# Pooled attention and a two-layer network on one core: one level of Strassen's scheme in the first product

## The chip, the core and the metric

The kernel runs on one core of one Trainium2 chip. Metric: device microseconds of one execution. The kernel before takes 949.67 us, the median of three runs (948.38 to 950.49). Engines are named as in the profile: PE multiplies matrices, PEld is its loading of the stationary operand, DVE, ACT and POOL work on vectors, SP issues the transfers.

## The reference, cut to what matters

Eight batches of eight heads, 576 positions, 64 features a head; keys and values are averaged over groups of 8 positions. The attention's output is a matrix x of 4608 tokens by 512, and goes through a network of width 2048:

```python
h = x @ w_in                                   # 4608x512 times 512x2048: "the first product"
sp = np.maximum(h, 0.0) + np.log1p(np.exp(-np.abs(h)))
g = h * erf(sp)
return (g @ w_out).astype(np.float32)          # 4608x2048 times 2048x512: "the second product"
```

The kernel computes both products with split operands: a float32 matrix is cut into a high part (rounded to the type `fp32r`) and a low part (the rest), and three products of parts are added up: high by high, high by low, low by high.

## The kernel before, in words

Tokens are cut into nine chunks of 512 (`TC`), the width of 2048 into sixteen pieces of 128 (`ft`). Each weight comes as 64-bit floats (`wi`, `wo`), one piece of 128x512 in one transfer of 512 KB. `load_weights` turns it into a high and a low part: two ACT or POOL steps (lines 340, 345, 347), two DVE steps (349, 351), a rounding copy (302 on ACT or 303 on POOL) and a subtraction on POOL (356). All 32 converted pieces stay in on-chip memory for the rest of the run.

`job` does the attention for a block of up to 256 tokens, tile by tile of up to 128 tokens: scores (PE, line 431), maximum and subtraction (DVE 436, 452), exponential (ACT 456), sum (DVE 458), normalization (DVE or POOL 472: both of its operands are in on-chip memory), transposes (PE 479, 484), and the values' products (PE 510, 511), whose results are split into `xh` and `xl` (516, 518).

`pair` handles two steps, each a chunk and one `ft`. The first product has 12 matrix instructions of 512 columns (line 535: four blocks of the 512 features, three products of parts each). Its result is copied out of the bank (540 on DVE or 541 on ACT), goes through softplus and erf (553, 560, each after a load of an ACT table), is multiplied (563) and split again into `gh` and `gl` (565 on ACT; 568 on DVE or POOL). The second product has 12 matrix instructions as well (line 582); `gh` and `gl` are the stationary operand there, and it adds up over the sixteen `ft` in four banks. So first and second products take turns, 12 by 12, and a chunk has 192 of each. `store` writes a finished chunk through two buffers `f` (594, 595, 596).

The order of all this is laid down before the kernel runs. `Program.order` plans with a cost in ns for each operation, a priority and a limited number of buffers, and places each operation where it can start first; the engines then run their instructions in that order, and wait for each other by semaphores. While PE has nothing to do in the first 57 us of the plan, it inserts idle matrix instructions ("fillers", line 622). Up to `FILL` they stand where the plan has a gap.

Of the kernel before, what the change touches and what calls it, by code (L numbers as in the profile page):

```python
# [39 lines left out]
SHIFT = 4  # L40
B1 = 2
# [5 lines left out]
W_IN, W_OUT, L_DUE = -1.0, -2.0, 2.0  # L47
G2 = 5.0
ON_DVE = 2
CAP_H, CAP_O, CAP_ATT, CAP_CV = 2, 4, 4, 2  # L50
ON_ACT = (0,)
SLACK, BIAS = 30, 2000
# [3 lines left out]
SWITCH = 1300  # L56
C_ID = 0
# [37 lines left out]
class Buf:  # L95


    def __init__(self, pool, shape, dtype, tag, limits):
        self.args = (pool, shape, dtype, tag)
        self.limits = limits  # L100
        self.left = 0
        self.state = {}
        self.held = False
        self._ap = None

    @property
    def ap(self):
        if self._ap is None:
            pool, shape, dtype, tag = self.args
            self._ap = (pool() if callable(pool) else pool).tile(shape, dtype, tag=tag, name=tag)  # L110
        return self._ap


class Op:
    def __init__(self, eng, cost, prio, fn):
        self.eng, self.cost, self.prio, self.fn = eng, cost, prio, fn
        self.bufs, self.next, self.wait, self.ready = [], [], 0, 0.0
        self.set = None


class Program:
# [9 lines left out]
    SAME = {"PE": 0, "ACT": 130, "DVE": 130, "POOL": 105, "SP": 0}  # L131

    def __init__(self, capacity, window):
        self.ops, self.capacity, self.window, self.filler = [], capacity, window, None

    def op(self, eng, cost, prio, fn, reads=(), writes=(), hold=(), alt=None, funcs=None):
# [3 lines left out]
        o.set = funcs  # L140
# [23 lines left out]
        for d, flow in deps.items():  # L164
            d.next.append((o, flow))
            o.wait += 1
        self.ops.append(o)
        return o

    def order(self):  # L170
        free = {e: 0.0 for e in self.DELAY}
        free["SP"] = 2150.0
        slots = {t: [0.0] * n for t, n in self.capacity.items()}
# [6 lines left out]
        progress, out, loaded = 0.0, [], "sigmoid"  # L180
        spare = heapq.heappop(slots["banks"]) if self.filler else None
        for _ in self.ops:
            best = None
            for e, ops in avail.items():
                pick, ready = None, []
                for o in ops:
# [4 lines left out]
                    start += switch  # L191
                    need = {}
# [5 lines left out]
                    for t, k in need.items():  # L198
# [3 lines left out]
                        start = max(start, heapq.nsmallest(k, slots[t])[-1] + (DGE if e == "SP" else 0))  # L202
                    if ok and e != o.eng:
                        ok = start + o.choice[e][0] <= max(o.ready, free[o.eng]) + o.cost + BIAS
                    if ok:
                        ready.append((start, o.key, o, start - switch * (1 - TURN) + SLACK * o.prio))
# [4 lines left out]
            if best is None:  # L211
                raise RuntimeError("no operation can go on")
# [5 lines left out]
            if spare is not None and o.eng == "PE":  # L218
                if start > FILL:
                    heapq.heappush(slots["banks"], start)  # L220
# [5 lines left out]
            if o.eng == "PE":  # L226
                progress = max(progress, o.prio)
            for b in o.bufs:
                if not b.held:
                    b.held = True  # L230
                    for t in b.limits:
                        heapq.heappop(slots[t])
                b.left -= 1
                b.end = max(getattr(b, "end", 0.0), end)
                if not b.left:
                    for t in b.limits:
                        heapq.heappush(slots[t], b.end + 150)
# [10 lines left out]
            out.append(o)  # L248
        self.length = max(free.values())
# [11 lines left out]
def moe_attention(ctx: ExitStack, tc: tile.TileContext, cst, qa, kl, vl, wi, wo, out):  # L261
# [3 lines left out]
    if wide:  # L265
# [5 lines left out]
    sizes = {"xh": 2, "xl": 2, "raw": 2, "q": 2, "et": 1, "etb": 1,  # L271
             "s": 2, "m": 2, "z": 2, "bb": 1, "ks": 1, "vs": 1, "hs": 3, "y": 1, "f": 2, "gh": 3, "gl": 3}
    pools = {t: pool(t, n) for t, n in sizes.items()}
    banks = pool("banks", 8, space=PSUM)
    sizes.update({"banks": 8, "h": CAP_H, "o": CAP_O, "att": CAP_ATT, "cv": CAP_CV})
# [3 lines left out]
    def buf(tag, shape, dtype=F32):  # L279
        return Buf(pools[tag], [P] + shape, dtype, tag, [tag])  # L280

    def bank(kind):
        return Buf(banks, [P, 512], F32, "banks", ["banks", kind])

# [7 lines left out]
    def gps(n):  # L292
        return 2.5 * n + 110

    def both(pool_too, cost, pool_cost, prio, fn, *access):

        op("DVE", cost, prio, lambda: fn(nc.vector), *access,
           alt=("POOL", pool_cost, lambda: fn(nc.gpsimd)) if pool_too else None)

    def copy(pool_too, n, prio, dst, src, *access, scale=1.0):  # L300

        op("ACT", act(n), prio, lambda: nc.scalar.activation(dst(), src(), AF.Copy, scale=scale), *access,
           alt=("POOL", 0.833 * n + 161, lambda: nc.gpsimd.tensor_scalar(
               out=dst(), in0=src(), scalar1=scale, scalar2=0.0, op0=ALU.mult, op1=ALU.add)) if pool_too else None)

# [9 lines left out]

    weights = pool("weights", 1)
    sizes.update({f"{n}{ft}": 1 for n in ("wi", "wo") for ft in range(NJ)})
    pieces = lambda n: [Buf(weights, [P, 2, 512], F32R, f"{n}{ft}", [f"{n}{ft}"]) for ft in range(NJ)]
    w_in, w_out = pieces("wi"), pieces("wo")
# [5 lines left out]
    def f32(ap):  # L325
        return ap.bitcast(F32)

    def load_weights(src, w, due):

        n = 512  # L330
        f, raw = buf("f", [n]), Buf(weights, [P, n, 2], U32, w.args[3], w.limits)
        words = lambda i: raw.ap[:, :, i]
        wh, wl = (lambda: w.ap[:, 0]), (lambda: w.ap[:, 1])
        if wide:


            op("SP", 1900, due - 6, lambda: nc.sync.dma_start(raw.ap.rearrange("p f w -> p (f w)"), src), [], [raw])
# [4 lines left out]

            low = buf("hs", [n], U32)
# [9 lines left out]
        else:  # L353
            op("SP", 950, due - 6, lambda: nc.sync.dma_start(f.ap, src), [], [f])
        copy(True, n, due - 2.5, wh, lambda: f.ap, [f], [(w, 0)])
# [307 lines left out]
```

## Time and profile before

| | |
|---|---|
| median of the runs shown | 949.67 us |
| profiled execution, own time | 950.75 us |
| its span | 949.0 us |
| PE busy | 928.5 us, 98% |
| ACT busy | 632.7 us, 67% |
| DVE busy | 445.9 us, 47% |
| POOL busy | 282.9 us, 30% |
| moved by the transfers | 58.55 MB |

The span is from the first to the last instruction; 1.75 us of the execution lie around it. A matrix instruction is pipelined: the next one starts before the last has ended, so what a matrix instruction costs is read from the distance between starts, not from its own duration. Idle time of an engine that nobody waits for costs nothing.

### The profile page before, as it was taken

The numbers are of one execution on the slowest core, as the hardware profiler recorded it, in microseconds if no ns is written. First come the engines' busy times: TensorE is split into PE (matmuls) and PEld (weight loads), VectorE is DVE, ScalarE is ACT, GpSimd is POOL, SyncE is SP. The second block draws the span as 40 slices with busy tenths as digits, with TensorE's granted clock in tenths as the row PEclk, the third lists the DMA queues.
The fourth block names the chain that finished last, engine by engine and source line by source line (L and its number), as shares of the span: only waits on it lengthen the run. The fifth ranks groups of instructions, "written<-read, shape, count | busy, mean of one in ns | idle before, by whom it ended". The sixth has DMA issues, their size and how long they took to land.

```text
span 949.0 us, 12377 instructions
## 1 busy us (share of the span) xinstructions
PE 928.5 (98%) x4485; PEld 767.2 (81%) x4485; DVE 445.9 (47%) x873; ACT 632.7 (67%) x1028; POOL 282.9 (30%) x400
## 2 busy tenths in 40 slices
PE   8999989999999999999999999999999999999997
PEld 6787767888888888888888888888888888888886
DVE  6987775543454444443455444434444443323331
ACT  5888775866675666766666667766666666666653
POOL 2689874241045301451132502242111010101000
PEclk9999999999999999999999999999999999999999
DMA  7892212310032100310021101120100010001001
GB/s 263 292 403 104 80 45 62 94 35 12 12 100 71 31 12 23 117 50 12 6 95 56 46 12 56 61 67 17 51 23 12 12 45 1 1 1 45 1 1 45
DMA packets 30349, 58.55 MB, mean 62 GB/s; under 512 B 7120, under 2 KB 7248, under 8 KB 30288
## 3 DMA queue, kind: packets, MB, share of 16 engines
q1 hardware_dynamic: 30288, 57.75, 18.5%
q8 instruction: 36, 0.59, 0.3%
q14 instruction: 25, 0.20, 0.1%
HBM read 48.30 MB, written 9.44 MB: 61 GB/s over the span
## 4 chain that ended last, share of the span: by engine, by line
PE 86%; DVE 1%; ACT 1%; DMA 0%; issue 0%; POOL 0%; ACTq 0%
PE banks L582 39%; PE banks L535 38%; PE banks L431 3%; PE banks L510 3%; PE banks L479 1%; PE banks L511 1%; DVE s L472 0%; PE banks L484 0%; DMA out<-f 0%; ACT hs L345 0%; ACT L553 0%; DVE m L436 0%; DVE s L452 0%; ACT y L553 0%; ACT banks L340 0%
## 5 line engine op out<-in xcount | busy, mean ns | idle before, releaser
L535 PE MATMUL banks<-xh,wi 128*128 128x512 f32 x1152 | 382.3, 393 | 1.4 <-DVE y L563 1.3
L582 PE MATMUL banks<-wo,gh 128*128 128x512 f32 x1152 | 362.0, 395 | 0.0
L535 PEld LDWEIGHTS banks<-xh,wi 128*128 128x128 f32 x1152 | 217.8, 189 | 48.8 <-DVE y L563 2.8
L582 PEld LDWEIGHTS banks<-wo,gh 128*128 128x128 f32 x1152 | 210.5, 188 | 42.4 <-issue 1.2
L535 PE MATMUL banks<-xl,wi 128*128 128x512 f32 x576 | 225.4, 391 | 0.0
L582 PE MATMUL banks<-wo,gl 128*128 128x512 f32 x576 | 224.9, 390 | 0.0
L541 ACT COPY hs<-banks 128x512 f32<-128x512 f32 x89 | 52.2, 586 | 202.1 <-PE banks L535 200.7
L568 DVE TENSOR_TENSOR gl<-hs,gh 128x512 fp32r<-128x512 f32 x78 | 55.3, 711 | 175.7 <-ACT gh L565 173.3
L582 PEld LDWEIGHTS banks<-wo,gl 128*128 128x128 f32 x576 | 108.1, 188 | 23.5
L535 PEld LDWEIGHTS banks<-xl,wi 128*128 128x128 f32 x576 | 108.9, 189 | 22.5
L568 POOL TENSOR_TENSOR gl<-hs,gh 128x512 fp32r<-128x512 f32 x50 | 64.6, 1292 | 184.6 <-ACT gh L565 174.4
L563 DVE TENSOR_TENSOR hs<-y,hs 128x512 f32<-128x512 f32 x128 | 87.7, 727 | 42.4 <-ACT y L560 42.2
L565 ACT CAST gh<-hs 128x512 fp32r<-128x512 f32 x128 | 78.6, 614 | 37.2 <-PE banks L582 32.7
L436 DVE TENSOR_REDUCE m<-banks 128x4 f32<-128x288 f32 (+1 forms) x80 | 36.2, 455 | 128.3 <-PE banks L431 127.2
L553 ACT ACT_TABLE_LOAD x72 | 92.4, 1283 | 1.8 <-PE banks L535 0.6
L560 ACT ACT_TABLE_LOAD x70 | 89.8, 1283 | 1.2
L494 POOL TENSOR_SCALAR etb<-etb 32x256 fp32r<-32x256 f32 (+1 forms) x40 | 22.4, 561 | 199.2 <-ACT etb L489 116.0
L560 ACT ACTIVATE y<-y 128x1024 f32<-128x1024 f32 (+1 forms) x73 | 76.5, 1049 | 0.8
L553 ACT ACTIVATE y<-hs 128x512 f32<-128x512 f32 x128 | 73.9, 625 | 0.7
L468 POOL TENSOR_TENSOR bb<-s,z 128x64 f32<-128x64 f32 (+1 forms) x40 | 12.2, 306 | 157.2 <-DVE z L462 149.3
L540 DVE COPY hs<-banks 128x512 f32<-128x512 f32 x39 | 27.0, 692 | 65.7 <-PE banks L535 65.7
L381 POOL TENSOR_TENSOR raw<-raw 128x256 f32<-128x256 f32 (+1 forms) x60 | 47.2, 790 | 25.0 <-DMA raw<-vl 13.3
(76 smaller groups left out, 935.5 us busy)
## 6 DMA issues: line engine op xcount, KB each, us to landing
raw<-vl SPq DMA_DIRECT2D x42, 256.0 KB, 2.8
out<-f SPq DMA_DIRECT2D x36, 256.0 KB, 2.0
raw<-kl SPq DMA_DIRECT2D x30, 288.0 KB, 3.1
wi<-wi SPq DMA_DIRECT2D x16, 512.0 KB, 8.1
wo<-wo SPq DMA_DIRECT2D x16, 512.0 KB, 9.4
q<-qa SPq DMA_DIRECT2D x28, 256.0 KB, 2.7
hs<-qa SPq DMA_DIRECT2D x4, 256.0 KB, 5.1
q<-qa SPq DMA_DIRECT2D x8, 128.0 KB, 2.5
```

What stands on the lines that cost most here:

```text
L381: op("POOL", gps(4 * size), prio, lambda: nc.gpsimd.tensor_add(t.ap[:, 0:4], t.ap[:, 0:4], t.ap[:, 4:8]), [t], [t])
L431: nc.tensor.matmul(o, raw.ap[:, p, :T], kbd[:, p], start=(pp == 0), stop=True, skip_group_check=True)
L436: op("DVE", dve(4 * SP), r + 0.4, lambda pv=pv, gs=gs: nc.vector.tensor_reduce(m.ap[:T, gs], pv(), AX.X, ALU.max), [ps], [(m, g)])
L510: nc.tensor.matmul(o, va[:, p], et.ap[:, p, :n], start=True, stop=False, skip_group_check=True)
L535: nc.tensor.matmul(ph.ap, w_in[ft].ap[:, w, P * p:P * p + P], x.ap[:, p, :], start=(p == 0 and q == 0), stop=(p == NP - 1 and q == 2))
L541: [ph], [hs[u]], alt=("ACT", act(TC, True), lambda u=u, ph=ph: nc.scalar.copy(hs[u].ap, ph.ap)))
L553: nc.scalar.activation(y.ap[:, half(k)], hh[k].ap, AF.Softplus)
L560: op("ACT", act(w), n + 1.9, lambda sl=sl: nc.scalar.activation(y.ap[:, sl], y.ap[:, sl], AF.Erf), own, own, funcs="sigmoid")
L563: op("DVE", dve(TC), n + 1.9, lambda k=k: nc.vector.tensor_mul(g(k), y.ap[:, half(k)], hh[k].ap), [(y, k), hh[k]], [gs[k]])
L565: op("ACT", act(TC), n + 2.0, lambda k=k: nc.scalar.copy(gh[k].ap, g(k)), [gs[k]], [gh[k]])
L568: e.tensor_sub(gl[k].ap, g(k), f32(gh[k].ap))
L582: nc.tensor.matmul(o[t].ap, g.ap[:, gs], w_out[ft].ap[:, w], start=(ft == 0 and q == 0), stop=(ft == NJ - 1 and q == 2))
```

## The change

Chunk 0 is computed as before, but with all sixteen `ft` of the first product ahead of the second product. The other eight chunks go in four pairs. Let A11, A12 be the two halves (256 features each) of the weights of piece i, and A21, A22 those of piece i+8; B11, B21 the two halves of the features of the pair's first chunk, B12, B22 those of its second. One level of Strassen's scheme in Winograd's form computes the four blocks of the result with seven products of half the depth where eight would be needed (`quad`, eight for each pair of chunks). Each of the seven is 6 matrix instructions of 512 columns: 42 for a quad, where the kernel before has 48.

- The sums of weights (S1 to S4, `sums`) and of features (T1 to T4, `sides`) are formed in float32 and then split into high and low parts. The attention's result is therefore kept in float32 (`xr`), and split later, in `limbs`.
- Five additions for each quad put the products together, all on DVE (`add`, line 733), with one operand in a bank; the first block of the four is read out of its bank directly by softplus.
- Softplus and erf take four blocks at once, so that the ACT tables change half as often.
- The second product is a phase of its own, after the eight quads of a pair, and transposed: the weights are the stationary operand and the tokens the moving one. It has 12 matrix instructions for each `ft` and chunk, as before. The result is written transposed, and the host turns it round.
- Weights no longer stay on the chip. Once converted, the parts are written to main memory (`raw_hbm`, `in_hbm`, `sum_hbm`, `out_hbm`), and every use loads them anew in pieces of 256 KB, high and low parts (`piece`, 14 places): seven for a quad, and two for each step of the second product.
- Buffers: 87 places of 2 KB a partition for all kinds of tile, instead of a pool for each.
- The planner now also counts POOL and those DVE operations marked `port` as one resource that only one of them can use at a time.

```diff
+NQ = NJ // 2
+FIRST, LONG, SHORT, PERIOD = 17.5, 14.0, 20.5, 34.5
+CAPS = {"g": 32, "x": 28, "xr": 11, "w": 14, "ws": 8, "w0": 36, "gl": 8, "t": 6, "f": 3, "q": 2, "q0": 4, "f0": 14, "v": 3, "vm": 1, "low": 2, "sw": 8,
+        "h": 6, "o": 4, "att": 4, "cv": 2, "dl": 3}
...
+                    if e == "POOL" or (e == "DVE" and o.port):
+                        start = max(start, port)
...
+    def halves(src, hi, lo, prio, reads, hikey, lokey, n=512, turn=None):
+
+        copy(True, n, prio, hi, src, reads, [hikey], [lokey[0] if isinstance(lokey, tuple) else lokey], turn=turn)
+        both(True, dve(n), gps(n), prio + 0.1, lambda e: e.tensor_sub(lo(), src(), f32(hi())),
+             reads + [hikey], [lokey])
...
+    def load_in(ft, due):
+
+        f, hi, lo = convert(wi[ft], due)
+        op("SP", 720, due + STORE, lambda: nc.sync.dma_start(raw_hbm[ft], f.ap), [f], [RAW[ft]])
+        a = slice(0, 2) if ft < NQ else slice(1, 2)
+        for l, w in enumerate((hi, lo)):
+            op("SP", 720 if ft < NQ else 360, due + STORE + 1, lambda l=l, w=w: nc.sync.dma_start(
+                f32(in_hbm[ft][:, a, l]), f32(w.ap).rearrange("p (a f) -> p a f", a=2)[:, a]), [w], [(IN[ft], l)])
...
+    def piece(src, kept, due, shape=(2, 256)):
+
+        w = place("w", F32R, shape)
+        op("SP", 720, due - 2, lambda: nc.sync.dma_start(f32(w.ap), f32(src())), [kept], [w], turn="w")
+        return w
...
+    def sides(s, due):
...
+                less(b[k], a[k], t1, q, sl, u)
+                less(b[2 + k], b[k], t3, q + 0.1, sl, u)
+                less(b[2 + k], t1, t2, q + 0.2, sl, u)
+                limbs("T2", k, t2, q + 0.3, sl, u)
+                limbs("T3", k, t3, q + 0.4, sl, u)
+                limbs("T1", k, t1, q + 0.5, sl, u)
+                less(a[2 + k], t2, t4, q + 0.6, sl, u)
+                limbs("T4", k, t4, q + 0.7, sl, u)
+                limbs("B22", k, b[2 + k], q + 0.8, sl, u)
...
-            def gemm1(ph=ph, ft=ft, xh=xh, xl=xl):
-                for p in range(NP):
-                    for q, (w, x) in enumerate(((0, xh), (0, xl), (1, xh))):
-                        nc.tensor.matmul(ph.ap, w_in[ft].ap[:, w, P * p:P * p + P], x.ap[:, p, :],
-                                         start=(p == 0 and q == 0), stop=(p == NP - 1 and q == 2))
...
+        p1, v, u = place("t"), place("t"), place("t")
...
+        product(A, a11, "B11", False, False)
+        out_of_bank(512, due + 0.3, lambda: p1.ap, lambda: A.ap, [A], [p1])
+        product(Bk, s2, "T2", False, True)
+        add(v, p1, Bk, due + 0.6)
+        product(C, s3, "T3", False, False)
+        add(u, v, C, due + 0.8)
+        product(Dk, s1, "T1", False, False)
+        add(g[1, 1], u, Dk, due + 1.0)
+        product(C, a22, "T4", True, True)
+        add(g[1, 0], v, C, due + 1.6)
+        product(A, a12, "B21", True, True)
+        product(Dk, s4, "B22", True, True)
+        add(g[0, 1], v, Dk, due + 1.8)
...
+    def second(ck, k, due, weights):
...
+            def gemm(j0=j0, o=po[ck]):
+                for j in (j0, j0 + 1):
+                    sl = slice(P * j, P * j + P)
+                    three(o[j].ap, (wh.ap[:, sl], wl.ap[:, sl]), (gh.ap, gl.ap), k == 0, k == NJ - 1)
```

**Three places in the order.** The first is PE in chunk 0. Before, PE has done the first product of two pieces of `wi` (`wi_545` is the second), and then the values' products of a block take turns with 53 fillers (one LDWEIGHTS and one MATMUL each) until the third piece comes:

```order
L535 MATMUL banks<-xh,wi_545 128x512
L510 MATMUL banks<-et,va 128x64
L511 MATMUL banks<-etb,vb 64x64
L510 MATMUL banks<-et,va 128x64
L511 MATMUL banks<-etb,vb 64x64
L622 LDWEIGHTS cst
L622 MATMUL banks<-cst 128x256
```

Now, from the first piece (high part `w_506`, low part `w_529`) to the second and third, there are no fillers in between:

```order
L664 MATMUL h<-x,w_506 128x512 x2
L664 MATMUL h<-x,w_529 128x512
L664 MATMUL h<-x,w_519 128x512 x2
L664 MATMUL h<-x,w_557 128x512
...
L664 MATMUL h<-x,w_613 128x512 x2
L664 MATMUL h<-x,w_627 128x512
```

What moved: 53 fillers that stood after PE's first matrix instruction of the first product are gone, and the conversion of `wo` has moved behind that of `wi`.

The second place is DVE at the start of the first pair, between its first product (which needs only B11) and its second (which needs T2, the end of the chain through `xr`). Line 638 forms the T's, line 349 the low parts (`x` of features, `ws` of weight sums), line 576 belongs to the last tile of attention, 430 and 431 to the sums of weights, 733 is the first addition of a quad:

```order
L576 TENSOR_TENSOR etb<-att,etb 32x128 x2
L431 TENSOR_TENSOR sw<-sw 128x256
L430 TENSOR_TENSOR sw<-sw 128x256
L638 TENSOR_TENSOR xr<-xr 128x128 x2
L638 TENSOR_TENSOR xr<-xr 128x384 x2
L638 TENSOR_TENSOR xr<-xr 128x128 x2
L638 TENSOR_TENSOR xr<-xr 128x384
L349 TENSOR_TENSOR x<-xr,x 128x384 x3
L638 TENSOR_TENSOR xr<-xr 128x128 x2
L638 TENSOR_TENSOR xr<-xr 128x384
L349 TENSOR_TENSOR x<-xr,x 128x128 x2
```

Nothing of this stands in the order before; there, DVE only splits the attention's result (line 518, one instruction for each values' product). What moved: the T's and their low parts now stand between the last tile of attention and PE's next product.

The third place is SP. Before, from chunk 2 on, it issues nothing but the attention's inputs and the outputs:

```order
L420 DMA q<-qa 128x512 x4
L596 DMA out<-f 128x512 x4
L375 DMA raw<-kl 128x576 x4
L420 DMA q<-qa 128x512
L375 DMA raw<-vl 128x512 x6
```

Now, in the first product of the second pair, the weights of each quad (`wi` the plain parts, `ws` the sums), and then those of the second product with the attention's inputs between them:

```order
L444 DMA w<-wi_84 128x512
L444 DMA w<-wi_92 128x512
L444 DMA w<-ws_140 128x512
L505 DMA q<-qa 128x512
L444 DMA w<-wo_141 128x512 x2
L460 DMA raw<-kl 128x576
L444 DMA w<-wo_149 128x512 x2
```

What moved: the whole program issues 765 transfers with 206.6 MB instead of 189 with 57.7 MB, all in SP's one queue.

More of the change, by code (lines that the diff above doesn't have):

```diff
@@ L56 @@
 SWITCH = 1300
+PLACES = 87
 C_ID = 0
@@ L166, in op @@
             o.wait += 1
+        if turn is not None:
+            if turn in self.turns:
+                self.turns[turn].follow.append(o)
+                o.wait += 1
+            self.turns[turn] = o
         self.ops.append(o)
@@ L179, in order @@
                     avail[e].append(o)
-        progress, out, loaded = 0.0, [], "sigmoid"
-        spare = heapq.heappop(slots["banks"]) if self.filler else None
+        todo = [(o.prio, i, o) for i, o in enumerate(self.ops) if o.eng == "PE"]
+        heapq.heapify(todo)
+        progress, out, loaded = todo[0][0], [], "sigmoid"
+        spare = None
+        if self.filler:
+            spare = heapq.heappop(slots["bank"])
+            self.idle.place = spare[1]
         for _ in self.ops:
@@ L225, in order @@
             end = free[o.eng] = start + o.cost
-            if o.eng == "PE":
-                progress = max(progress, o.prio)
+            if e == "POOL" or (e == "DVE" and o.port):
+                port = end
+            o.done = True
+            while todo and todo[0][2].done:
+                heapq.heappop(todo)
+            progress = todo[0][0] if todo else progress
             for b in o.bufs:
@@ L236, in order @@
                     for t in b.limits:
-                        heapq.heappush(slots[t], b.end + 150)
+                        heapq.heappush(slots[t], (b.end + 150, b.places[t]))
+            for d in o.follow:
+                d.wait -= 1
+                if not d.wait:
+                    for a in d.choice:
+                        avail[a].append(d)
             for d, flow in o.next:
@@ L388, in job @@
             for p in range(NP):
-                load_pool(kl[b, p], ks, p, SP, base + KEYS + KEYS_R * p, "s" if first and p > 1 else "raw")
+                load_pool(kl[b, p], ks, p, SP, base + KEYS + KEYS_R * p, "raw")
             for r0, c0 in ((64, 0), (0, SP)):
@@ L501, in job @@
             at += T
-        xh, xl = xtile(ck)
         xs = slice(off, off + n)
+        plain = ck == 0
+        if ck not in xt:
+            if plain:
+                xt[ck] = [(place("x", F32R), place("x", F32R)) for _ in range(NP)]
+            else:
+                xt[ck] = [place("xr") for _ in range(NP)]
         for p in range(NP):
@@ new lines, in three, with activation, softplus @@
+    def three(o, w, x, first, last):
+        (wh, wl), (xh, xl) = w, x
+        for q, (u, v) in enumerate(((wh, xh), (wh, xl), (wl, xh))):
+            nc.tensor.matmul(o, u, v, start=first and q == 0, stop=last and q == 2, skip_group_check=True)
+    def activation(hs, prio):
+        ys = [buf("d", [2, 512]) for _ in range(2)]
+        y = lambda k: ys[k // 2].ap[:, k % 2]
+        own = [(ys[k // 2], k % 2) for k in range(4)]
+        def softplus():
+            for k, (h, _) in enumerate(hs):
+                nc.scalar.activation(y(k), h.ap, AF.Softplus)
+        op("ACT", 4 * act(512), prio, softplus, [h for h, _ in hs], own, funcs="softplus")
+        for k in range(2):
+            op("ACT", act(1024), prio + 0.2, lambda k=k: nc.scalar.activation(ys[k].ap, ys[k].ap, AF.Erf),
+               own[2 * k:2 * k + 2], own[2 * k:2 * k + 2], funcs="sigmoid")
+        for k, (h, g) in enumerate(hs):
+            if g is h:
+                both(True, dve(512), gps(512), prio + 0.3, lambda e, k=k, h=h: e.tensor_mul(
+                    h.ap, y(k), h.ap), [own[k], h], [h])
+            else:
+                op("DVE", dve(512), prio + 0.3, lambda k=k, h=h, g=g: nc.vector.tensor_mul(
+                    g.ap, y(k), h.ap), [own[k], h], [g])
@@ L592, in store @@
-    def store(ck, t, o, prio):
-        ot, r0 = buf("f", [DM]), TC * ck + P * t
-        op("ACT", act(512, True), prio, lambda: nc.scalar.copy(ot.ap, o.ap), [o], [ot],
-           alt=("DVE", dve(512), lambda: nc.vector.tensor_copy(ot.ap, o.ap)))
-        op("SP", 800, prio, lambda: nc.sync.dma_start(out[r0:r0 + P, :], ot.ap), [ot], [])
-    steps = [(ck, ft) for ck in range(NC) for ft in range(NJ)]
-    loads = sorted([(ft + W_IN, wi[ft], w_in[ft]) for ft in range(NJ)]
-                     + [(ft + G2 + W_OUT, wo[ft], w_out[ft]) for ft in range(NJ)], key=lambda w: w[0])
@@ L603, in moe_attention @@
+    gs, po = {}, {}
+    order = [i + NQ * m for i in range(NQ) for m in range(2)]
+    start = lambda s: FIRST + PERIOD * (s - 1)
+    jobs = {}
     for ck, b, tiles, off, fresh in blocks():
```

350 lines of the change are left out of this document (217 added, 133 removed).

## The prediction

> **What bounds the kernel now.** I read the page's first two parts, then a table of stretches with the busy time of each engine, then the chain of waits at the end, which gives the price of a matrix instruction.
>
> ```profile
> PE 928.5 (98%) x4485; PEld 767.2 (81%) x4485; DVE 445.9 (47%) x873; ACT 632.7 (67%) x1028; POOL 282.9 (30%) x400
> ...
> 200.00:400.00 200.00, 200.00 (x956) 165.91 (x955) 87.45 (x178) 133.13 (x210) 54.53 (x80) 1.00 0.14 42
> 250.00:930.00 680.00, 680.00 (x3204) 564.11 (x3203) 282.62 (x556) 444.85 (x674) 146.47 (x216) 1.00 0.11 36
> ...
> 928.70 13.61 PE banks L582 x60
> ```
>
> The columns of a stretch are PE, PEld, DVE, ACT and POOL busy, the granted clock, the share of the transfer engines and GB/s. From 250 to 930 us PE is never idle, at full clock, and no other engine is busy for more than 65%. So there the time is PE's work and nothing else. In the last chain 60 matrix instructions take 13.61 us: **226.8 ns each**. The first product, the second product and the attention's scores in the same stretch:
>
> ```profile
> 39.39:150.00 110.61, 49.14 (x191) 37.30 (x192) 0.97 0.47 167
> 250.00:930.00 680.00, 323.64 (x1343) 251.21 (x1341) 1.00 0.11 36
> ...
> 39.39:150.00 110.61, 35.71 (x144) 26.54 (x144) 0.97 0.47 167
> 250.00:930.00 680.00, 337.29 (x1339) 247.04 (x1340) 1.00 0.11 36
> ...
> 39.39:150.00 110.61, 7.97 (x48) 6.37 (x48) 0.97 0.47 167
> 250.00:930.00 680.00, 29.53 (x200) 26.11 (x200) 1.00 0.11 36
> ```
>
> The 2682 instructions of both products take 608.3 of the 680 us. The other 71.7 us are attention, 25 tiles by their 200 score instructions: **2.87 us a tile**.
>
> The first 150 us are different. PE's first product starts at 39.39 us. Until 150.0 it does 336 instructions (76.2 us) and 6 tiles (17.2 us) in 110.6 us, so **17.2 us are lost** there. The rows below show where.
>
> ```profile
> 50.24 3.67 PE L622 MATMUL banks<-cst 128*128 128x256 bf16 x32
> ...
> 60.90:150.00 89.10, 79.98 (x354) 63.67 (x354) 64.50 (x113) 70.22 (x106) 71.00 (x90) 0.96 0.35 118
> ...
> 120.33 1.31 POOL L356 TENSOR_TENSOR wo<-f,wo 128x512 fp32r<-128x512 f32 x1
> 120.42 0.69 DVE L351 SCALAR_TENSOR_TENSOR f<-wo,banks 128x512 uint32<-128x512 uint32 x1 [0.48 <-POOL wi L356]
> 122.44 1.27 POOL L356 TENSOR_TENSOR wo<-f,wo 128x512 fp32r<-128x512 f32 x1
> 122.52 4.42 DVE L472 TENSOR_TENSOR s<-s,z 64x576 f32<-64x576 f32 x1
> 124.64 1.27 POOL L356 TENSOR_TENSOR wo<-f,wo 128x512 fp32r<-128x512 f32 x1
> 125.87 0.45 POOL L383 TENSOR_TENSOR raw<-raw 128x128 f32<-128x128 f32 x1
> 128.18 0.43 PE L479 MATMUL banks<-cst,s 64*128 64x64 f32 x4 [3.01 <-DVE s L452]
> 129.41 0.63 PE L535 MATMUL banks<-xl,wi 128*128 128x512 f32 x1
> 129.84 1.05 PE L535 MATMUL banks<-xh,wi 128*128 128x512 f32 x2
> L472 DVE TENSOR_TENSOR s<-s,z x34: 741/759/4423, 55.7 to 804.1; 128x576 f32<-128x576 f32 x27, 64x576 f32<-64x576 f32 x7
> ```
>
> PE idles in fillers before the third weight, since conversion isn't ready. Later POOL is the busiest engine (71.0 of 89.1 us) and DVE gets stuck behind it: line 472, with both operands on chip, takes 759 ns in the median and 4.42 us while POOL has no gap, whereas line 351, with one operand in a bank, takes its 0.69 us beside a running POOL instruction. PE then stands for 3.01 us, and its next instructions start 0.43 us apart (129.41 to 129.84) for 3.4 us: a stall of that length costs about 1.7 us more.
>
> **The change, term by term.** The sum is made on the span, 949.0 us; the profiled execution's own time is 1.75 us more, the median shown 0.67 us more, and I use the median.
>
> *Removed.* The order has 1344 instructions in the pairs' first products instead of 1536, 192 in chunk 0 and 1728 in the second product as before. PE has 192 fewer by 226.8 ns: **-43.5 us**. The transposed product has operands of the same size, so the same price. No row of before has steady products beside transfers at a high rate (36 GB/s from 250 to 930); that arriving weights slow PE's step is possible, and I charge nothing for it.
>
> *End.* Now two buffers `f` hold the last stores up:
>
> ```profile
> 943.27 0.39 PE L582 MATMUL banks<-wo,gl 128*128 128x512 f32 x1
> 944.39 0.59 ACT L594 COPY f<-banks 128x512 f32<-128x512 f32 x1 [2.15 <-DMA out<-f]
> 945.31 0.59 ACT L594 COPY f<-banks 128x512 f32<-128x512 f32 x1 [0.33 <-DMA out<-f]
> ```
>
> The last copy ends at 945.90. With a third buffer and one copy each on ACT and DVE it ends some 0.9 us after PE's 943.66: **-1.3 us**.
>
> *Start and first pair.* Ahead of the first product the order has the same work on DVE, ACT and SP, so I leave 39.39 us as it is. Then four sections, priced by these rows (mean ns of one behind the busy time):
>
> ```profile
> L568 DVE TENSOR_TENSOR gl<-hs,gh 128x512 fp32r<-128x512 f32 x78 | 55.3, 711 | 175.7 <-ACT gh L565 173.3
> L568 POOL TENSOR_TENSOR gl<-hs,gh 128x512 fp32r<-128x512 f32 x50 | 64.6, 1292 | 184.6 <-ACT gh L565 174.4
> L303 POOL TENSOR_SCALAR wi<-f 128x512 fp32r<-128x512 f32 x13 | 8.5, 655 | 1.3 <-DVE f L351 1.0
> L381 POOL TENSOR_TENSOR raw<-raw 128x256 f32<-128x256 f32 (+1 forms) x60 | 47.2, 790 | 25.0 <-DMA raw<-vl 13.3
> L518 DVE TENSOR_TENSOR xl<-banks,xh 128x256 fp32r<-128x256 f32 (+3 forms) x96 | 32.6, 351 | 14.7 <-ACT xh L516 13.6
> ...
> 5.00:10.00 5.00, 4.73 (x37) 3.70 (x34) 2.59 (x4) 0.86 (x2) 0.00 (x0) 1.00 1.03 353
> ```
>
> 1. Instructions 1 to 48 (10.9 us of PE): only `wi` is converted, the fillers are gone. Between 10.9 and 13; I take 12, since DVE has 11.8 us of work here.
> 2. 49 to 384, the rest of chunk 0: PE has 76.2 us and 8 tiles, 99.2 us. POOL has 32 subtractions at 1.29 (41.3), 22 rounding or byte steps at 0.66 (14.4) and 32.9 us of pooling and small steps: 88.6. DVE's operations with both operands on chip add 18.4 (11 of 512 columns, 4 normalizations, 5 of 384, the rest small). If these exclude POOL as at 122.52, that is 107.0 us in a row. Before, from 60.9 to 150, the same two kinds filled some 80 of 89.1 us, 90%; at 90% this section takes 119. Bounds 99 and 119; I take 113, for the planner now keeps the two apart, yet ACT (90.8) and DVE (92.1) are nearly as full.
> 3. The first 48 of pair 1: PE has 10.9 and 1.9 us. Its second product waits for T2. DVE, whose queue holds the T's, low parts and weight sums, has 18 low parts of 128 or 384 columns (7.0), 9 of weight sums (3.4), 13 T's (4.9), 5 additions (3.5), 7 sums (2.7) and 0.9 besides: 22.4 us, and POOL little. Bounds 13 and 24; 22.5, since PE waits for that very queue.
> 4. The next 96: PE 21.8 us. The queue has 10.0 MB, stores of weights included; at the 353 GB/s of the saturated row it needs 28.3. Bounds 21.8 and 29; 25, as nobody waits for most of the stores.
>
> Lost in the four: 1.1 + 13.8 + 9.7 + 3.2 = 27.8 us, against 17.2 before: **+10.6 us**.
>
> A rule of the Trainium skill bears on section 2, the page "SBUF — State Buffer", section "Who interferes with whom": a DVE instruction with two SBUF inputs and a GpSimd instruction that reads SBUF exclude each other for their whole length, others do not. The trace agrees (4.42 us at line 472, 0.69 at line 351). By the rule section 2 can't be shorter than 107.0; without it 99.2 would do and the forecast be 14 us lower.
>
> *The quads.* Each has five additions with a bank as operand, and the fifth product writes into the bank that the second addition must have read. From the third product's last start that addition ends 0.39 + 0.04 + 0.69 us later, by these rows:
>
> ```profile
> 922.87 0.39 PE L535 MATMUL banks<-xh,wi 128*128 128x512 f32 x1
> 923.30 0.69 DVE L540 COPY hs<-banks 128x512 f32<-128x512 f32 x1 [1.15 <-PE banks L535]
> ```
>
> The fourth product covers 0.23 + 1.36 us. That leaves some 0.4, unless an unrelated DVE instruction of 0.7 us is ahead. Bounds 0 and 0.7 us a quad; with 0.1, 32 quads give **+3.2 us**. In a pair's first product (76.2 us) ACT has 7.5 us a quad of 9.5, so the activation stays hidden, with half the table loads; its cover is the next quad.
>
> *Streaming.* A pair issues 41.2 MB, 117 us at 353 GB/s, of 189 us of PE (720 x 0.2268 + 9 tiles). Fourteen places hold 19 us of work ahead; a transfer lands in 2 to 10 us here:
>
> ```profile
> raw<-vl SPq DMA_DIRECT2D x42, 256.0 KB, 2.8
> wo<-wo SPq DMA_DIRECT2D x16, 512.0 KB, 9.4
> ```
>
> Nothing is charged. Stores and inputs of attention are queued behind the pieces, and they wait in turn; the same 19 us cover that.
>
> Sum: 949.67 - 43.5 - 1.3 + 10.6 + 3.2 = 918.7, so **919 us**. Its own range, 909 to 930, comes from 103 to 119 in section 2 and 0 to 0.25 us a quad.
>
> **Rivals.**
>
> *The start costs no more than before.* Section 2 at its 107 and 3 at 22 us, with nothing lost in 1, 4 and the quads: lost 7.8 + 9.2 = 17, as before: 949.67 - 44.8 = 905 us. For it: the planner's new exclusion. Against it: no section before ran at full use of its busiest engine.
>
> *The start eats most of it.* 13, 119, 24 and 29: lost 2.1 + 19.8 + 11.2 + 7.2 = 40.3, and 0.35 us a quad, 11.2: 949.67 - 44.8 + 23.1 + 11.2 = 939 us. For it: POOL, DVE, ACT, PE and the queue are all within 15% of one another in section 2, and each stall over 3 us halves the clock.
>
> *Streaming binds, slower than before.* One queue in order, 206.6 MB instead of 57.7, stores mixed in. PE waits once the queue yields under 41.2 MB / 189 us = 218 GB/s, and all is lost under 208 (9 us more a pair, in 3.5 pairs). At half the row of 353, 234 us a pair: 919 + 3.5 x 45 = about 1077. Against it: 353 in the row at 5 us, with lines of 2 KB; for it only that no row before holds a mix of reads and writes at such a rate.
>
> That PE's instructions don't get fewer is excluded by the order.
>
> **How the numbers follow.** Forecast 0.50, costless start 0.21, costly start 0.21, streaming 0.06, and 0.02 for a result between 940 and 950 by several of these. Range 904 to 940: it takes in both starts and leaves out the streaming. Measurements of this kernel tell 0.2% (2 us) from no change. Faster 0.92, same 0.02, slower 0.06.
>
> **What would show it.** PE 3264 instructions of 512 columns at 227 ns; PE busy throughout a later pair, and a pair's period near 189 us; DVE in a row of instructions with PE idle for about 10 us at the start of pair 1; POOL and DVE nearly full in chunk 0. I am wrong if PE waits for `w` pieces in pairs 2 to 4, if each quad has a gap over 0.3 us, or if the first product starts much later than 39 us.

## The result, and the profile after

The changed kernel takes **914.78 us** in the median of four runs (912.97 to 915.98), the kernel before 949.56; the ratio is 0.9633, with a 95% interval of 0.9612 to 0.9653. The forecast was 919, its range 904 to 940. The profiled execution took 915.39 us, with a span of 913.6. Of all executions in this document one was far slower, one of the six of experiment 7 (1269.57 us, at a mean granted clock of 0.653 where the others have 0.99); the ratios leave it out, and without it that median is 909.0 instead of 909.1 us.

The first part of the page, then the product instructions in the stretches of the prediction's sections (from the first to the 49th, 385th, 433rd, 529th and the last one; the columns are PE, PEld, clock, share of the transfer engines, GB/s), and the end of the chain:

```profile
PE 890.5 (97%) x4250; PEld 729.2 (80%) x4250; DVE 554.6 (61%) x1036; ACT 507.4 (56%) x898; POOL 415.1 (45%) x538
```

```profile
40.06:51.05 10.99, 10.99 (x49) 9.10 (x50) 1.00 0.48 167
51.05:158.95 107.90, 84.79 (x337) 62.20 (x336) 0.98 0.89 303
158.95:186.05 27.10, 16.50 (x48) 11.76 (x49) 0.75 1.00 352
186.05:208.10 22.05, 22.05 (x98) 18.02 (x96) 1.00 0.95 353
208.10:909.39 701.29, 650.42 (x2737) 506.36 (x2735) 1.00 0.60 205
```

```profile
744.37 77.37 PE h L664 x336
821.73 88.07 PE o L664 x384
```

Three things are to be seen. The start (the first four rows) takes 168.0 us, of which 27.1 belong to the first 48 instructions of pair 1. From 208 us on PE never stands still: the eight quads of the last pair are one row of 336 instructions without a gap. And that row gives 230.3 ns for an instruction, the second product 229.3, where the row that gave the price had 226.8. Streamed weights land in a median of 5.3 us, and PE has no wait for them among its waits:

```profile
w<-wo SPq DMA_DIRECT2D x256, 256.0 KB, 5.3
w<-wi SPq DMA_DIRECT2D x96, 256.0 KB, 5.2
w<-ws SPq DMA_DIRECT2D x96, 256.0 KB, 5.3
```

At the start of pair 1 PE and DVE stand as follows (timeline, the start and the time of a row, in brackets the idle time ahead and what ended it):

```profile
166.53 0.79 PE L664 MATMUL h<-x,ws 128*128 128x512 f32 x1 [2.14 <-ACT x L337]
169.13 1.65 PE L664 MATMUL h<-x,ws 128*128 128x512 f32 x3 [1.81 <-DVE x L349]
171.37 5.36 PE L664 MATMUL h<-x,ws 128*128 128x512 f32 x14 [0.59 <-DVE x L349]
178.89 4.55 PE L664 MATMUL h<-x,w 128*128 128x512 f32 x12 [2.17 <-issue]
```

```profile
164.31 2.29 DVE L638 TENSOR_TENSOR xr<-xr 128x128 f32<-128x128 f32 x7
166.52 1.48 DVE L349 TENSOR_TENSOR x<-xr,x 128x384 fp32r<-128x384 f32 x3
...
171.03 2.54 DVE L349 TENSOR_TENSOR x<-xr,x 128x128 fp32r<-128x128 f32 x5
...
175.72 1.42 DVE L349 TENSOR_TENSOR ws<-sw,ws 128x256 fp32r<-128x256 f32 x4
...
178.11 0.68 DVE L733 TENSOR_TENSOR t<-t,h 128x512 f32<-128x512 f32 x1
```

DVE goes from T's to low parts to weight sums to the quad's first additions, PE waits for this row four times (the first time by way of ACT, which rounds the T's), and the clock is at half for half of the section (mean 0.75). The last of the four waits, ahead of the fifth product, ends 0.10 us after the second addition (178.11 + 0.68 us). That addition must have read the bank into which the fifth product writes, and it stands in DVE's row behind the weight sums. The profile names no releaser for it ("issue").

### The profile page after: what moved, and what is told of

It reads as the page before. It is cut to its first block, busy times and chain, and to the rows that moved or that the text cites. A ratio compares the mean times of both kernels' runs of the same rounds, so it can differ in the third digit from the quotient of the medians.

```text
span 913.6 us, 13356 instructions
## 1 busy us (share of the span) xinstructions
PE 890.5 (97%) x4250; PEld 729.2 (80%) x4250; DVE 554.6 (61%) x1036; ACT 507.4 (56%) x898; POOL 415.1 (45%) x538
## 4 chain that ended last, share of the span: by engine, by line
PE 88%; DVE 4%; POOL 4%; issue 2%; DMA 1%; ACT 1%; SPq 0%; POOLq 0%; DVEq 0%; ACTq 0%
PE o L664 42%; PE h L664 35%; PE att L516 4%; PE att L599 3%; PE h L816 2%; PE att L564 2%; POOL w L349 1%; PE att L600 1%; DMA v<-vl 1%; POOL low L390 1%; DVE f L394 1%; DVE x L349 0%; DMA wi<-w 0%; PE att L569 0%; DVE xr L638 0%
## 5 line engine op out<-in xcount | busy, mean ns | idle before, releaser
L664 PE MATMUL o<-gl,w 128*128 128x512 f32 x1728 | 425.3, 396 | 0.0
L664 PEld LDWEIGHTS o<-gl,w 128*128 128x128 f32 x1728 | 315.7, 188 | 67.6 <-issue 1.0
L664 PE MATMUL h<-x,w 128*128 128x512 f32 x1344 | 315.8, 395 | 5.2 <-DVE g L685 3.0
L664 PEld LDWEIGHTS h<-x,w 128*128 128x128 f32 x1344 | 254.0, 189 | 62.3 <-DVE g L685 3.4
L682 POOL TENSOR_TENSOR g<-d,g 128x512 f32<-128x512 f32 x54 | 69.6, 1306 | 192.5 <-ACT d L678 192.5
L733 DVE TENSOR_TENSOR g<-t,h 128x512 f32<-128x512 f32 x96 | 65.9, 686 | 61.0 <-PE h L664 59.4
L349 POOL TENSOR_TENSOR gl<-g,gl 128x512 fp32r<-128x512 f32 x62 | 87.4, 1410 | 33.0 <-ACT gl L337 31.6
L337 ACT ACTIVATE gl<-g 128x512 fp32r<-128x512 f32 x119 | 70.8, 623 | 19.8 <-DVE g L685 17.3
L733 DVE TENSOR_TENSOR t<-t,h 128x512 f32<-128x512 f32 x64 | 43.9, 687 | 56.3 <-PE h L664 50.4
L678 ACT ACTIVATE d<-d 128x1024 f32<-128x1024 f32 x72 | 72.5, 1053 | 0.4
L349 DVE TENSOR_TENSOR gl<-g,gl 128x512 fp32r<-128x512 f32 x82 | 57.3, 721 | 13.9 <-ACT gl L337 9.9
L343 ACT COPY f<-o 128x512 f32<-128x512 f32 x21 | 12.2, 587 | 84.9 <-PE o L664 84.7
```

The costliest lines, as they stand in the source:

```text
L343: op("ACT", act(n, True), prio, lambda: nc.scalar.copy(dst(), src()), *access, alt=("DVE", dve(n), lambda: nc.vector.tensor_copy(dst(), sr ...
L349: both(True, dve(n), gps(n), prio + 0.1, lambda e: e.tensor_sub(lo(), src(), f32(hi())), reads + [hikey], [lokey])
L664: nc.tensor.matmul(o, u, v, start=first and q == 0, stop=last and q == 2, skip_group_check=True)
L678: op("ACT", act(1024), prio + 0.2, lambda k=k: nc.scalar.activation(ys[k].ap, ys[k].ap, AF.Erf), own[2 * k:2 * k + 2], own[2 * k:2 * k + 2 ...
L682: both(True, dve(512), gps(512), prio + 0.3, lambda e, k=k, h=h: e.tensor_mul(h.ap, y(k), h.ap), [own[k], h], [h])
L733: op("DVE", dve(512), prio, lambda: nc.vector.tensor_add(dst.ap, u.ap, o.ap), [u, o], [dst])
```

## The experiments

All times are medians; "the change" is 914.78 us.

**1. Eight products instead of seven.** The quad computes the four blocks directly:

```diff
-        product(Bk, s2, "T2", False, True)
-        add(v, p1, Bk, due + 0.6)
...
+        for j, (w, m, half) in enumerate(((a11, 0, 1), (a12, 0, 2), (a21, 1, 1), (a22, 1, 2))):
+            for t in range(2):
+                product(h[m, t], w, f"B{half}{t + 1}", half == 2, half == 2)
```

> The scheme alone is undone: eight half products of plain operands in each quad (48 instructions instead of 42), no T's, no sums of weights, no additions; the four results are copied out of their banks. Phases, streamed weights and transposed second product stay. Theory A (the gain is the count of PE's instructions, less what the T's cost at the start): 192 instructions more at 0.2297 us are +44.1 us, and the first 48 of pair 1 fall from 27.1 to some 18 us, -9; 914.8 + 35 = 950 us. Theory B (a good part of the gain comes from what goes along with it, fewer table loads and weights no longer kept): clearly under 940 us. Theory C (the scheme's start costs far more than the first 48 show): over 955 is excluded, and the time is near 914.8 + 44.1 - 20 = 939 us.

Measured: **949.38 us**, a ratio of 1.0002 to the kernel before (0.9988 to 1.0016). The first stretch is that from the start of pair 1 to its 49th product instruction, with all engines (PE, PEld, DVE, ACT, POOL); the other row is the first product of the last pair.

```profile
158.96:175.45 16.49, 15.35 (x67) 12.09 (x66) 2.61 (x8) 4.25 (x12) 1.90 (x5) 0.90 0.97 333
```

```profile
767.32 88.34 PE h L654 x384
```

48 instructions more take 10.97 us in the last pair (88.34 against 77.37), 228.5 ns each; the start of pair 1 is 10.6 us shorter without the T's. So theory A holds: 44.1 less 10.6 is 33.5 of the 34.6 us between the two kernels. And all that goes along with the scheme (streaming, the transposed product, fewer table loads, the new planner) comes to nothing in sum, within the interval's 1.5 us: the whole gain is the scheme's.

**2. The planner without the shared resource.**

```diff
-                    if e == "POOL" or (e == "DVE" and o.port):
-                        start = max(start, port)
```

> The planner no longer counts POOL and the marked DVE operations as one resource; nothing else is changed. Theory A (they do exclude each other on the chip): DVE's operations with two on-chip operands get stuck behind POOL, their mean rises (0.72 us now for 512 columns), and the first matrix instruction to the end of pair 1's first 144 takes 5 to 15 us longer than its 168.0: 920 to 930 us. Theory B (the exclusion binds only in the plan): the plan is 6 us shorter without it, so 909 us, with unchanged means.

Measured: **922.83 us**, 8.0 us more than the change. The groups of DVE in the change, then in this kernel (lines are two lower there):

```profile
L733 DVE TENSOR_TENSOR g<-t,h 128x512 f32<-128x512 f32 x96 | 65.9, 686 | 61.0 <-PE h L664 59.4 <-DMA w<-wi 0.7 <-DMA w<-wo 0.7
L349 DVE TENSOR_TENSOR gl<-g,gl 128x512 fp32r<-128x512 f32 x82 | 57.3, 721 | 13.9 <-ACT gl L337 9.9 <-DMA w<-wo 2.5 <-POOL gl L338 1.2
L349 DVE TENSOR_TENSOR x<-xr,x 128x512 fp32r<-128x512 f32 (+2 forms) x57 | 34.6, 639 | 0.7 <-POOL x L338 0.4
L557 DVE TENSOR_TENSOR s<-s,z 128x576 f32<-128x576 f32 (+1 forms) x32 | 32.7, 1023 | 11.8 <-POOL bb L553 11.5
```

```profile
L347 DVE TENSOR_TENSOR gl<-g,gl 128x512 fp32r<-128x512 f32 x86 | 70.8, 846 | 16.3 <-ACT gl L335 11.5 <-POOL gl L336 3.8 <-DMA w<-wo 0.5
L731 DVE TENSOR_TENSOR g<-t,h 128x512 f32<-128x512 f32 x96 | 65.9, 687 | 62.5 <-PE h L662 61.3 <-DMA w<-ws 0.7
L555 DVE TENSOR_TENSOR s<-s,z 128x576 f32<-128x576 f32 (+1 forms) x34 | 42.6, 1252 | 10.3 <-POOL bb L551 9.9
L347 DVE TENSOR_TENSOR x<-xr,x 128x512 fp32r<-128x512 f32 (+2 forms) x41 | 40.8, 1026 | 2.2 <-POOL x L336 1.4 <-ACT x L335 0.7
```

Operations with both operands on chip get slower (721 to 846 ns, 639 to 1026, 1023 to 1252), those with one in a bank don't (686 and 687). The means with "forms" mix shapes; of one shape alone, 128x512 of `x` goes from 717 to 1238 ns and 128x576 of `s` from 906 to 1125. The first 528 product instructions take 174.3 us instead of 168.0. The plan promised 6 us less, the chip gave 8 more: theory A.

**3. Without the T's.**

```diff
-                less(b[k], a[k], t1, q, sl, u)
...
-                limbs("T4", k, t4, q + 0.7, sl, u)
+                limbs("T2", k, b[k], q + 0.3, sl, u)
```

> The T's of every pair are left out, and with them their low and high parts: one split of B12 stands in for T1 to T4, so the result is another. PE's instructions stay. Theory A (at the start of pair 1 PE waits for DVE's queue of T's, low parts and sums): the first 48 of pair 1 fall from 27.1 us to 17 to 19, the total by some 9 to 905 us; later pairs unchanged at 189.6. Theory B (PE waits there for the last tile of attention, whose values' products start at 161.7, and for the halved clock): at most -3 us, 912.

Measured: **905.25 us**, 9.5 less. The start of pair 1 in the change, then here:

```profile
158.95:186.05 27.10, 18.78 (x67) 13.72 (x66) 23.59 (x59) 14.55 (x39) 7.83 (x11) 0.75 1.00 352
```

```profile
158.71:174.49 15.78, 13.79 (x68) 10.90 (x67) 11.76 (x31) 9.07 (x22) 7.03 (x11) 1.00 1.00 353
```

DVE's 23.59 us become 11.76, the section 15.78, and the clock stays full. Theory A, with a larger effect than it gave. Of the 11.3 us, 6.3 are idle time of PE and 5.0 its busy time, which is shorter at the full clock, so this experiment doesn't part DVE's row from the clock; the next one tries to.

**4. Fillers in PE's waits.**

```diff
+                    if idle and k == 0:
+                        idle_on(idle, 20)
...
+            if idle and q == 0:
+                idle_on(idle, 16)
```

> 36 idle matrix instructions of 107 ns are put into PE's waits in the second product of the first quad of pair 1 (20 ahead of it, 16 behind its first instruction), 3.9 us of the 8.3 us that PE stands still there. Theory A (the row of DVE's work sets this section, whatever PE's clock): the section stays at 26 to 28 us, the total at 914 to 915. Theory B (the stalls halve the granted clock from 165.2 to 175.4 us, and this costs up to 5 us more): the clock stays full, the section falls to 22 or 23, the total to 910.

Measured: **918.37 us**, 3.6 more. The section takes 27.90 us:

```profile
162.22:190.12 27.90, 21.75 (x104) 16.99 (x103) 23.60 (x59) 14.31 (x39) 7.57 (x11) 0.82 0.99 351
```

```profile
182.26 5.26 PE L670 MATMUL h<-x,w 128*128 128x512 f32 x12 [4.02 <-issue]
```

The mean clock rose from 0.75 to 0.82, but the wait ahead of the fifth product grew from 2.17 to 4.02 us, and ends again 0.10 us after DVE's second addition: DVE's row takes 23.60 us as before, and PE only waits elsewhere. Theory A for the section, though the clock didn't stay full as theory B supposed, so its case wasn't reached. Of the rest, 1.2 us more until the first product and 2.1 in the stretch up to pair 1 (a second spell of half clock at 132.6) lie ahead of the edit, where the order is the same on every engine; why they came in this program stays open.

**5. Weights not streamed.**

```diff
+        if (shape, turn) not in once:
+            w = once[shape, turn] = place("w", F32R, shape)
...
+        return once[shape, turn]
```

> Each of the three kinds of weight piece is loaded once and held, and every product uses it, so the result is another; PE's, DVE's, ACT's and POOL's instructions stay, and 445 of the 448 loads of 256 KB are gone. Theory A (streaming is hidden entirely, and the mean distance between product instructions, 229.7 ns instead of 227.5 before, has nothing to do with it): 913 to 915 us. Theory B (transfers into on-chip memory beside PE stretch each product instruction by those 2.2 ns): 2736 of them from 208 us on give 6.0 us, so 908 to 909 us, with a distance of 227.5 ns. Theory C (the loads also hold up the start, where the queue was full): the first 48 of pair 1 under 25 us.

Measured: **913.47 us** (911.55 to 914.93), which the spread of both doesn't tell from the change. From 400 to 800 us the transfers fell to 33 GB/s, and the last pair's rows are

```profile
743.21 77.36 PE h L666 x336
820.57 87.61 PE o L666 x384
```

230.2 and 228.2 ns. Streaming 117 MB (448 pieces) beside the products costs some 1 us (1.3 by the medians) or nothing, and isn't what slowed them: theory A. Experiments 7 and 8 say the same from the other side: they stream all of it, at 226.7 ns. The start of pair 1 takes 27.1 us here too, so it isn't the queue either.

**6. Without the low parts of wo.**

```diff
+            lo = hi
+            copy(True, n, due - 2.5, lambda: hi.ap, lambda: f.ap, [f], [hi])
```

> The low parts of the sixteen pieces of wo aren't formed (the high part is used in their place, so the result is another); this takes 16 subtractions, 11 on POOL at 1.32 us and 5 on DVE at 0.7, out of the stretch between matrix instructions 49 and 384, and nothing from PE, ACT or SP. Theory A (POOL and DVE's two-operand work in a row set that stretch, 106.9 of 107.9 us): it falls by 7 to 9 us to PE's own 99 to 101, the total to 906. Theory B (no single engine sets it; short waits for DVE and ACT, 82 and 87 of 108 us busy, do): at most -3 us there, 912 to 915.

Measured: **910.91 us**. The stretch from instruction 49 to 384 in the change, then here:

```profile
51.05:158.95 107.90, 101.43 (x501) 83.20 (x500) 86.61 (x171) 82.06 (x150) 84.75 (x110) 0.98 0.89 303
```

```profile
50.91:154.27 103.36, 100.20 (x501) 81.87 (x500) 79.58 (x163) 75.28 (x136) 86.28 (x120) 1.00 0.90 316
```

4.5 us less, between both theories, and the experiment doesn't part them: the planner filled POOL up again (84.75 to 86.28 us) with what DVE and ACT had done, and both of these fell by 7 us. POOL's time and that of DVE's instructions marked `port`, added up from the trace, fell by just 5.5 us (106.9 to 101.4).

**7. Other addresses.** The small buffers are allocated ahead of the 87 places, which in the change are mixed with them in order of first use:

```diff
+    for o in made_order:
+        for b in o.bufs:
+            if b.home != "bank" and b.home != "u" and b.home not in seen:
+                seen.add(b.home)
+                for i in range(sizes[b.home]):
+                    space.tile([P, room[b.home]], F32, tag=f"{b.home}{i}", name=f"{b.home}{i}")
     for o in made_order:
         o.fn()
```

> The same order and instructions; only the addresses differ: the small buffers are placed first, so that all 87 places start at one remainder modulo 2 KB and from 45 KB up (now some lie between 12 and 36 KB, at other remainders). In the trace of the change, instructions with an operand in those low places start 231 to 233 ns apart, the rest 228.9. Theory A (the place of the operands costs this): mean distance 228.9 or less, total -2 to -3 us, 912. Theory B (chance: the low places are those used at certain times): no change in mean distance, 914 to 915.

Measured: **909.10 us**, ratio to the kernel before 0.9572 (0.9559 to 0.9584): 5.7 us less than the change, by addresses alone. The last pair:

```profile
738.72 76.16 PE h L664 x336
814.88 87.05 PE o L664 x384
```

226.7 ns in both products, the price of the kernel before. That kernel has its product operands at one remainder too, the same as here: 960 bytes modulo 2 KB. The gain is more than theory A gave; what about the addresses does it, the next three tell in part.

**8. Low addresses.** The places come first, from 7 KB up, all at one remainder modulo 2 KB (960 bytes again):

```diff
+    for i in range(PLACES):
+        space.tile([P, 512], F32, tag=f"u{i}", name=f"u{i}")
```

> As the kernel with the new addresses (909.1 us, 227.5 ns between product instructions), but the 87 places come first, from 7 KB up, and the small buffers behind them; all places still start at one remainder modulo 2 KB. Theory A (what slows is a mixture of remainders among the operands' places): 227.5 ns, 909 us. Theory B (what slows is an operand below 36 KB): about 10% of the places lie there, as in the change itself, so 229 to 230 ns, 914 us.

Measured: **908.89 us**.

```profile
740.38 76.16 PE h L664 x336
816.54 87.05 PE o L664 x384
```

**9. Mixed remainders.** As experiment 7, with a gap ahead of every eighth place:

```diff
+        if i % 8 == 0:
+            space.tile([P, 8 if i % 16 else 16], F32, tag=f"gap{i}", name=f"gap{i}")
+        space.tile([P, 512], F32, tag=f"u{i}", name=f"u{i}")
```

> As the kernel with the new addresses, all places above 45 KB, but a gap of 32 or 64 bytes is left ahead of every eighth place, so that they start at eleven remainders modulo 2 KB. Theory A (mixture of remainders): the distance is 229.7 ns or more, the total 914 to 920 us. Theory B (only operands below 36 KB are slow): 227.5 ns, 909 us.

Measured: **922.37 us**, 13.3 more than experiment 7.

```profile
750.08 78.05 PE h L664 x336
828.13 89.06 PE o L664 x384
```

**10. Gaps of 64 bytes only.**

```diff
-            space.tile([P, 8 if i % 16 else 16], F32, tag=f"gap{i}", name=f"gap{i}")
+            space.tile([P, 16], F32, tag=f"gap{i}", name=f"gap{i}")
```

> As the kernel with mixed remainders (922.4 us, 232.1 ns), but all eleven gaps are 64 bytes, so that every place starts at the same remainder modulo 64 and at eleven different ones modulo 2 KB. Theory A (any mixture of remainders modulo 2 KB slows): 232 ns, 922 us. Theory B (only steps of 32 bytes among the places do, the grain is 64 bytes): 227.5 ns, 909 us.

Measured: **919.01 us**.

```profile
747.23 77.86 PE h L664 x336
825.09 88.90 PE o L664 x384
```

Low addresses don't slow (226.7 ns); places at different remainders do, 232.3 and 231.9 ns with steps of 32 bytes among them, 231.7 and 231.5 with steps of 64. That is what theory A gave in all three, but a rival is left that none of them tests: wherever it is fast, the one remainder is 960 bytes, and none of the eleven is 960. So the runs don't tell whether mixing slows, or every remainder other than 960.

**11. Every piece twice.**

```diff
+        x = spare[len(spares) % 16]
+        op("SP", 720, due - 2, lambda: nc.sync.dma_start(f32(x), f32(src())), [kept], [], turn="w")
```

> Behind every weight piece the same 256 KB are transferred once more, to main memory, where nobody reads them; nothing waits for these. A pair then moves 72.7 MB instead of 41.2. At the 353 to 388 GB/s that full stretches show this takes 187 to 206 us, beside PE's 189.6, and SP needs 0.71 us for an issue (6 in 4.27 us), some 280 issues a pair, 199 us. Theory A (streaming has this margin of nearly two and no more): pairs of 195 to 210 us, total 935 to 985 us, with PE waiting for w. Theory B (the margin is larger): 915 to 920 us. Theory C (the margin is far smaller, because reads and writes mixed run slower): over 1000 us.

Measured: **947.38 us** (942.76 to 952.85). Pairs 2 and 3 take 206.6 and 200.5 us. A stretch of them, with all engines, and PE's waits for pieces:

```profile
500.00:700.00 200.00, 193.09 (x894) 155.26 (x893) 117.95 (x206) 105.16 (x173) 71.06 (x97) 0.99 0.98 356
```

```profile
PE o L670 <- DMA w<-wo: 8.3, 11, 2.2
PE h L670 <- DMA w<-wi: 6.1, 8, 1.2
```

The transfer engines are at 0.98 with 356 GB/s, and 72.7 MB a pair by that rate are 204 us: theory A. SP's issuing isn't the limit: its 274 issues in this stretch take 129 of the 200 us, 0.47 us each and not the 0.71 that was expected. The change needs 205 GB/s, so it has a margin of 1.7.

**12. The best of these.** Experiment 7, and the weight sums of pair 1 due one unit later:

```diff
-        got = sums(i, due) if s == 1 else None
+        got = sums(i, due + 1) if s == 1 else None
```

> The kernel with the new addresses, and the weight sums of pair 1 get a due time later by one unit, so that the planner places T's and their parts ahead of them. The plan is 2.0 us shorter, all of it in the first 48 of pair 1 (25.5 us in the kernel with the new addresses). Theory A (what stands in DVE's row ahead of the T's is what PE waits for): that section falls by 2 to 4 us, the total from 909 to 905 to 907. Theory B (the sums are only late instead, in the next 96): no change in the sum of both sections, 909 us.

Measured: **906.18 us**, ratio to the kernel before 0.9543 (0.9529 to 0.9557): faster than the change, and than experiment 7, though the two intervals only just don't overlap. The start of pair 1 is 1.6 us shorter than in experiment 7 (25.52 us), and the next 96 take 21.76 in both:

```profile
159.04:182.99 23.95, 16.04 (x68) 12.07 (x66) 23.08 (x52) 13.12 (x36) 11.08 (x14) 0.79 0.97 336
```

That is theory A for the total. The section itself fell by less than the 2 to 4 us that theory A gave.

## Why the prediction was right, term by term

The sum came out 4 us too high, and closer than its terms deserve:

| term | predicted | measured |
|---|---|---|
| 192 instructions fewer | -43.5 | -43.5 by the old price |
| a dearer instruction from 208 us on | 0 | +7.9 (2736 x 2.9 ns) |
| attention's tiles from 208 us on | 0 | -4.6 |
| end | -1.3 | -1.5 |
| first product later | 0 | +0.7 |
| the four sections | +10.6 | +6.2 |
| gaps in the quads | +3.2 | 0 |
| streaming | 0 | 0 to 1 |
| sum | -31.0 | -34.8 (of the spans: -35.4) |

*Removed.* Right in the count and nearly in the price: experiment 1 gives 228.5 ns for each of the extra ones. "The transposed product has operands of the same size, so the same price" was the step that failed by a little: size wasn't all. Neighbouring product instructions from 208 us on start 229.7 ns apart in the mean, 2.9 more than my price. Measured the same way, over neighbours from 250 us on, the kernel before has 227.5, so 0.7 of the 2.9 was in the price, which came from one short row, and 2.2 (6.0 us) is the change's. The text named arriving weights as a possible reason; experiment 5 rules these out, and experiments 7 to 10 show that it is where the operands lie. The tiles pay back a part: the 701.29 us from 208.10 on less 2736 x 0.2297 leave 72.8 us for 27 tiles, 2.70 each instead of 2.87. That is a difference of two sums, and no experiment was made on it. With 227.5 ns for the products of the kernel before its tiles come to 2.79, and some 2 of the 4.6 us are the same 0.7 ns again.

*Start.* The sections took 11.0, 107.9, 27.1 and 22.05 us, predicted were 12, 113, 22.5 and 25. Section 2 came out near the 107.0 us of POOL and DVE's two-operand work in a row, and in part by luck: the trace has 84.7 us of POOL instead of 88.6, and with 18.1 of DVE's two-operand work the row is 102.8 (106.9 with DVE's one-operand additions to `z`, which the planner marks as well). By the rule of the Trainium skill, "SBUF — State Buffer", section "Who interferes with whom", the section can't undercut that row. Experiment 2 agrees with the rule in every group of DVE with two on-chip operands of 384 columns or more; the small `vb<-vm,vb` went the other way (592 to 444 ns). The prediction's "others do not" goes further than that section of the Trainium skill, which lets DVE's 2-port modes contend with GpSimd too. In experiment 2 the one-operand `z<-z` of 128x8 went from 358 to 430 ns. That the row's sum also sets the section isn't shown: experiment 6 left it open, and in the trace the two engines together fill 87% of the stretch, since a waiting instruction's recorded time overlaps that for which it waits.

Section 3 was outside its bound of 24: experiments 1, 3 and 4 agree that PE waits there for DVE's row of T's, low parts and sums, as the text said. What I left out is that DVE waits for PE in turn: its row is 23.59 us, nearly the 22.4 of the sum, and 3.5 us are idle in between, 2.5 of them ahead of two additions whose product wasn't ready. And "each stall over 3 us halves the clock" was too narrow: here the clock was at half from 165.2 to 175.4 us, and the longest stall was 2.14 us. In section 4 the stores, which nobody waits for, cost nothing, as its lower bound had it.

*The quads.* 0.1 us a quad was a guess between 0 and 0.7; it is 0, for 336 instructions of the last pair stand in one row. Ahead of its additions DVE was idle for 59.4 and 50.4 us, waiting for PE (the groups in experiment 2 show the first of the two): it was early, and not late once from 208 us on. In the first quad of pair 1 it was late: the wait for the second addition there (2.17 us) is counted in section 3.

*Streaming.* Right, with its limit: experiment 11 reaches the row of 353 GB/s from the kernel before, at 356. The rival that mixed reads and writes run far slower falls, since that experiment mixed them too.

*The other rivals.* "The start costs no more than before" was wrong by 6.2 us, or 6.9 with the later first product, and its other half, no loss in the quads, was right; its 905 us are missed by these 6.9 and by 3.3 of dearer instructions less cheaper tiles. "The start eats most of it" is excluded: 23.4 us were lost, not 40.

## What to carry to other kernels

Where the trace shows one engine full, price a removed instruction from a long row of that engine: 192 of them came out within 1.1 us of what the whole kernel gained, once the start was counted. What the removal costs is paid where the covering work has not begun yet: look for the engine whose queue holds the new preparation in one row, and put ahead what is waited for. And look at addresses: a shared pool of equal places lost 5.7 us here when other buffers were allocated between them.

## What the runs showed of the hardware that I had not expected

The distance between product instructions depends on where the places of the operands start. With all places at 960 bytes modulo 2 KB it is 226.7 ns, from 7 KB up or from 45 KB up; in the change, where 336 of 3264 moving operands and 380 of the stationary ones lie at one of four other remainders, 229.3 to 230.3 in the last pair; with eleven remainders, none of them 960, 231.5 to 232.3. Per run that is 909 to 922 us with the same instructions in the same order. Within the change it goes by how many operands lie elsewhere: the first product of pair 2 has 54 of 672 elsewhere and takes 76.55 us (227.8 ns), those of pairs 3 and 4 have 84 and 96 and take 77.35 and 77.37 us (230.2 and 230.3). Transfers don't explain it (experiment 5). Nor does one bad place among the eleven: in experiment 9 the mean distance lies between 231.6 and 232.5 ns for every one of the remainders of the moving operand. It isn't only a matter of the single instruction either, since in the change those whose own operands and the next one's all lie at 960 still start 228.8 ns apart. Whether the mixture as such slows, or each remainder but 960, isn't shown: no run has all places at another single remainder. Starting every place at a multiple of 64 bytes doesn't cure it (experiment 10). Which grain would do, and what in the reading of operands causes it, stays open.
